# Products of a zero tile in the front of an S4 convolution and gated feed-forward kernel

## The chip, the cores and the metric

The kernel runs on one core of one Trainium2 chip. The metric is the device time of one execution in microseconds, as the median of three runs. A core has a matrix engine, TensorE (PE in the profile; its loading of the stationary operand is shown apart, as PEld), a vector engine (VectorE, DVE), an activation engine (ScalarE, ACT), a general engine (GpSimd, POOL) and an engine that here only starts transfers (SyncE, SP). They work side by side and wait for one another through semaphores. TensorE writes into PSUM, a small memory that DVE and ACT then empty; all else lies in SBUF, the on-chip working memory, and is loaded and stored by DMA. The profile also records which share of its full clock TensorE was granted.

## What is computed

The input is one sequence of 2048 tokens with 640 channels. Six modulation rows come from a small vector c. The first half of the block is a long convolution over the sequence (an S4 layer) on the normalised input, the second a gated feed-forward layer:

```
mod = silu(c) @ w_mod                    # six rows of 640: sa, ca, ga, sb, cb, gb
h = layernorm(x) * (1 + ca) + sa
K[d, l] = Re( sum_n C[d,n] * exp(dt[d] * A[d,n] * l) * dt[d] * B[d,n] )
y = causal_convolution(h, K) + h * Dskip # by FFT over 4096 points in the reference
x = x + ga * y
h = layernorm(x) * (1 + cb) + sb
x = x + gb * ((silu(h @ w1) * (h @ w3)) @ w2)
```

A, B and C are complex and have 128 states for each channel. w1 and w3 are 640 x 1728, w2 is 1728 x 640. All numbers are float32.

## The kernel before

The convolution is done as a transform in two stages over 32 x 64 points, with constant tables (s1r, s1, s2, i1, i2) as operands of matrix products. The kernel has three stretches.

**The front.** First come the parameters. `polar` (lines 236 to 296) turns A, B, C and dt of 128 channels, and later of the other 512, into exponents and phases; it turns its tables over by products with a unit matrix (L285) into `lx`. `mod_early` (line 305) is called eight times. Each call takes up to 256 columns of w_mod: `mod_sums` multiplies them by silu(c) on TensorE (L303, four column groups of 32), DVE copies the sums out (L311), TensorE turns the row into columns (L313), and DVE copies these into `cols` (L314). `mod_shift` (line 316) then makes the shift of the first layer norm: two groups of products (L327, L336) and their copies (L328, L338).

For each of the sixteen tiles of 128 tokens `ln1_norm` normalises the tile and `u_stage1` (line 413) does the first stage of the transform: products of 32 rows by 64 columns (L430), in every other tile also products of one row (L422) for the shift, into two PSUM tiles `pu`, one with the tag Z, one with A or B. ACT or DVE empties the first (L435), DVE the second (L436), and SP stores the result in the scratch `us` (L437).

Meanwhile the convolution's kernel K is made, in 40 steps of 16 channels. A step s consists of the phases on POOL (L487 to L489), absolute value, cosine and sine on ACT, exponents from TensorE (L451, tile `pa`) through ACT's exponential, real and imaginary tables on DVE (L516 to L527), the sum over the states on TensorE (`kgen`, L540, tile `pk`), its scaling on DVE (`k1evac`, L547 and L548), and the first stage of its transform on TensorE (`k_stage1`, L558, tile `pt`), which ACT copies out. The front runs ten rounds of a loop over these steps, `kgen` of step 0 to 8 among them.

**The rounds.** Behind the front the steps of K and the second stage (`stage2`, L589), the products in the frequency domain (L606 to L614) and the inverse (`inverse1`, L631) run in an order written out by hand, the string ROUND, with the flag `in_order[0]` set: each instruction is then held behind the one traced before it on its engine.

**The feed-forward layer** follows, with weights split into two parts of fewer bits and seven instead of eight block products. Its instructions are recorded by a helper and all carry L108. Between the convolution and this layer stands `keep_warm`: 10 and 18 products of a zero tile called `idle`, 128x128 by 128x512, into PSUM that nothing reads.

What sets the order in the front is a planner: it simulates the engines and issues what is ready first, except for what is pinned. `tc.keep_in_program_order` pins one instruction behind the one traced just before it on the same engine; what is traced after it is not pinned by that. ACT's instructions in the front are pinned, TensorE's are not. The planner also makes the waits: a tile in PSUM that is read waits for everything traced before that writes into its bank. A tile with a tag and one buffer waits for the readers of its predecessor with the same tag: Z, A and B serve `pu`, `pa`, `pT` and others, pk the sums of K, pb the `pt`, and pk and pb in turn the sums of `mod_early`.

The tile `dz`, 128 x 160, is cleared by DVE at the very start (L164). Later SP loads the 640 numbers of Dskip into four of its 128 rows (L765), and `k1evac` adds it to the sums. The products of the change read its first 128 columns as the stationary operand and its columns, 160 at most, as the moving one.

Of the kernel before, what the change touches and what calls it, by code (L numbers as in the profile page):

```python
# [9 lines left out]
F32 = mybir.dt.float32  # L10
# [7 lines left out]
P = 128  # L18
L = 2048
D = 640  # L20
F = 1728
NA, NB = 32, 64
DC = 128
NDC = D // DC
SD = 16
# [65 lines left out]
def bc(ap, axis, n):  # L91
    v = ap.unsqueeze(axis)
    shape = list(v.shape)
    shape[axis] = n
    return v.broadcast_to(shape)
# [18 lines left out]
def tile_kernel(ctx: ExitStack, tc: tile.TileContext, a):  # L114
    nc = tc.nc
    V, S, G, PE = nc.vector, nc.scalar, nc.gpsimd, nc.tensor
# [16 lines left out]
    in_order = [False]  # L133

    def keep(ins):

        return tc.keep_in_program_order(ins) if in_order[0] else ins
# [5 lines left out]
    def acopy(out, in_):  # L143
        return tc.keep_in_program_order(S.copy(out, in_))  # L144
# [17 lines left out]
    gaT = kp.tile([P, D // 4], F32, name="gaT")  # L162
    dz = kp.tile([P, D // 4], F32, name="dz")
    V.memset(dz, 0.0)  # L164
    sc = kp.tile([P, KD], F32, name="sc")
    one4 = kp.tile([P, 1], F32, name="one4")
    cT = kp.tile([P, KD], F32, name="cT")
# [2 lines left out]
    psS = ssm.enter_context(tc.tile_pool(name="psS", bufs=1, space=PSUM))  # L170

    tz = ctx.enter_context(tc.tile_pool(name="tz", bufs=4, reuse_waits="tile"))
    tabs = ExitStack()
    tp = tabs.enter_context(tc.tile_pool(name="tp", bufs=2, reuse_waits="tile"))
    once = lambda shape, dt, name: tp.tile(shape, dt, name=name, bufs=1)
# [122 lines left out]
    def mod_sums(w, pm):  # L298

        n = w.shape[2]  # L300
        for k in range(KD):
            g = slice(k % 4 * NA, k % 4 * NA + NA)
            keep(PE.matmul(pm[g, :n], sc[:, k:k + 1].broadcast_to([P, NA]), w[:, k, :], start=(k < 4), stop=(k > 0), tile_position=(0, g.start)))  # L303

    def mod_early(i, w, tag):

        pm = psS.tile([P, 512], F32, name="pm", tag=tag, bufs=1)
        n = w.shape[2]
        mod_sums(w, pm)
        part = flat[2 * (i % 2)][:, 6 * D:]  # L310
        V.tensor_copy(part[:, :n], pm[:, :n])  # L311
        for b in range(n // P):
            PE.matmul(pm[:, 256 + b:257 + b], part[:, b * P:(b + 1) * P], one4, start=True, stop=True)  # L313
        V.tensor_copy(cols.rearrange("p s k -> p (s k)")[:, 2 * i:2 * i + n // P], pm[:, 256:256 + n // P])  # L314

    def mod_shift():

        sa, ca, ga, zero, inv, r, gs = (cols[:, i] for i in range(7))
        V.tensor_scalar(ca, ca, 1.0, None, op0=OP.add)
        V.tensor_scalar(zero, ca, 0.0, 1e-18, op0=OP.is_equal, op1=OP.mult)  # L320
        V.tensor_tensor(ca, ca, zero, op=OP.add)
        V.reciprocal(inv, ca)
        V.tensor_tensor(r, inv, sa, op=OP.mult)

        pr = psS.tile([P, 2, 512], F32, name="pr", tag="Z", bufs=1).rearrange("p a b -> p (a b)")
        for k in range(KD):
            PE.matmul(pr[:64, k * P:(k + 1) * P], r[:, k:k + 1].broadcast_to([P, 64]), ident, start=True, stop=True)  # L327
        V.tensor_copy(rrow[:64], pr[:64, :D])  # L328
        rc = hpz.tile([P, 4, D // 2], F32, name="u")[:, 0].rearrange("p (k c) -> p k c", k=KD)
        V.tensor_tensor(rc, bc(c1, 1, KD), bc(r, 2, 2 * NA), op=OP.mult)  # L330
        ps = psS.tile([P, 512], F32, name="ps", tag="pk", bufs=1)
        for k in range(KD):
            for hh in range(2):
                lo, hi = max(k * P, hh * 320), min(k * P + P, hh * 320 + 320)
                if lo < hi:
                    PE.matmul(ps[hh * 64:hh * 64 + 64, lo - hh * 320:hi - hh * 320], rc[:, k],  # L336
                              ident[:, lo - k * P:hi - k * P], start=True, stop=True, tile_position=(0, hh * 64))
        V.tensor_copy(shift, ps[:, :320])  # L338

    def mod_gate():  # L340
# [72 lines left out]
    def u_stage1(j):  # L413


        x = xt[j]
        u = hpz.tile([P, 4, D // 2], F32, name="u", bufs=2)
        pu = [psS.tile([P, 2, 512], F32, name="pu", tag=t, bufs=1) for t in ("Z", "AB"[j % 2])]
        one = j % 2 == 0
        for q in range(2 if one else 0):  # L420
            for hh in range(2):
                PE.matmul(pu[0][hh * 64:hh * 64 + 64, q, :320], c1[q * NA:q * NA + 1],  # L422
                          rrow[q * NA:q * NA + 1, hh * 320:hh * 320 + 320],
                          start=True, stop=False, tile_position=(q * NA, hh * 64))
        for h in range(2):
            for q in range(2):
                r0 = (2 * h + q) * NA
                r = slice(r0, r0 + NA)
                for hh in range(2):
                    PE.matmul(pu[h][hh * 64:hh * 64 + 64, q, :320], s1r[r], x[r, hh * 320:hh * 320 + 320],  # L430
                              start=not (one and h == 0), stop=True, tile_position=(r0, hh * 64))
        if one:
            acopy(u[:, :2, :], pu[0][:, :, :320])
        else:
            V.tensor_tensor(u[:, :2, :], pu[0][:, :, :320], bc(shift, 1, 2), op=OP.add)  # L435
        V.tensor_tensor(u[:, 2:, :], pu[1][:, :, :320], bc(shift, 1, 2), op=OP.add)  # L436
        nc.sync.dma_start(usw[:, 4 * j:4 * j + 4, :], u)  # L437
# [95 lines left out]

    def kgen(s):
        E, A = EC.pop(s), AA.pop(s)
        pk = psS.tile([P, SD // 4, NB], F32, name="pk", tag="pk", bufs=1)
        for g in range(SD // 4):
            for st, x in enumerate((E, A)):
                for dq in range(4):
                    keep(PE.matmul(pk[dq * 32:dq * 32 + 32, g, :], x[:, g * 4 + dq, 1, :], x[:, g * 4 + dq, 0:3:2, :],  # L540
                                   start=(st == 0), stop=(st == 1), tile_position=(0, dq * 32)))
        PK[s] = pk

    def k1evac(s):
# [178 lines left out]
    def conv_part(fn):  # L723
        return lambda k: fn((k - LAG) // 8, (k - LAG) % 8)

    parts = {"PH": phases, "AB": absph, "CO": cosine, "SI": sine, "PA": lambda k: exp_fast((k,)), "XA": fast,
             "PQ": lambda k: exp_slow((k,)), "XQ": slow, "E1": real1, "E2": real2, "A1": imag1, "A2": imag2,
             "kg": kgen, "K": k1evac, "pt": k_stage1, "uk": k_out}
    conv = {"st": conv_part(stage2), "kc": conv_part(k_copy), "T": conv_part(products), "Y": conv_part(sums),
            "iv": conv_part(inverse1), "zt": conv_part(z_store)}  # L730
# [30 lines left out]
    for i, t in enumerate(("pb", "pk", "pb", "pk", "pb")):  # L761
        mod_early(i, wm[i], t)
# [4 lines left out]
    for j in range(4, 7):  # L767
        ln1_load(j)
    nc.sync.dma_start(prm[:, :, d1], prma[:, :, d1])
    mod_shift()  # L770
    exps(0)
    ln1_norm(0)
# [3 lines left out]
    for n in ("AB", "CO", "SI"):  # L776
        do(n, 0)
    u_stage1(0)
    u_stage1(1)
    ln1_norm(2)  # L780
    for i, t in enumerate(("pb", "pk", "pb")):
        mod_early(5 + i, wg[i], t)
    mod_gate()
    u_stage1(2)
    u_stage1(3)
    rest = polar(d1, G)
# [61 lines left out]
    for rnd in range(NS // EB):  # L848
        if 2 <= rnd < 7:
            late_load(rnd - 2)  # L850
        for word in ROUND:
            name, k = word[:2].rstrip("+-"), EB * rnd + int(word[len(word[:2].rstrip("+-")):])
# [51 lines left out]
    V, S, G, PE = (InOrder(tc, e, (in_order,)) for e in (V, S, G, PE))  # L904
# [544 lines left out]
```

## Time and profile before

| | us |
|---|---|
| median of three runs | 998.04 |
| the three runs | 998.29, 992.06, 998.04 |
| the profiled execution's own time | 1000.31 |
| its span, first to last instruction | 998.5 |
| PE, DVE, ACT, POOL busy in the span | 911.9, 737.4, 535.6, 340.6 |
| mean granted clock of TensorE over the span | 0.94 |

A line of the profile gives the start, the busy time, the engine, the source line, the operation, out and in by the program's names, and the shapes; brackets hold how long the engine was idle before and what ended that. A row of the view by stretches gives the stretch, its length, the busy time of each engine with its count of instructions, the granted clock, the mean busy share of the 16 DMA engines, and GB/s. A row of the view of waits gives the engine and line that waited, for whom, and then the sum, the number and the longest of the waits. A product of float32 numbers appears as two records. Ends of matrix products are modelled, their starts are not.

### The profile page before, as it was taken

What the parts mean: (1) busy time and instruction counts of PE and PEld (TensorE: products, weight loads), DVE (VectorE), ACT (ScalarE), POOL (GpSimd) and SP (SyncE); (2) the same over time, 40 slices, a digit from 0 to 9 for tenths busy, and PEclk for the clock granted to TensorE, in tenths of its full rate; (3) what the DMA queues carried; (4) which work ended last, traced back from release to release, by engine and by line L of the source; (5) the groups of instructions that cost most, each with busy time, mean ns of one, the idle gap of its engine ahead of it and who ended that gap; (6) DMA issues with size and microseconds to landing.
All of it is one profiled execution on the core that took longest, in us unless ns stands there. A gap on an engine that the chain in (4) does not pass through costs nothing.

```text
span 998.5 us, 19955 instructions
## 1 busy us (share of the span) xinstructions
PE 911.9 (91%) x7924; PEld 681.0 (68%) x7924; DVE 737.4 (74%) x1224; ACT 535.6 (54%) x732; POOL 340.6 (34%) x310
## 2 busy tenths in 40 slices
PE   5777788999989997889999999989899999999998
PEld 2434545666666665567888888666678888888786
DVE  4588868999999975678566676687796666676765
ACT  4559468999999942356333333354643333333332
POOL 1541242455544300323222233354342222224441
PEclk9956757999999999999999999999999999999999
DMA  9462264667765788691211104979231111123352
GB/s 261 151 246 89 117 152 137 170 198 209 196 182 173 207 198 246 204 280 48 92 54 54 53 28 118 253 217 280 69 131 54 54 54 53 53 87 99 93 200 76
DMA packets 103568, 140.67 MB, mean 141 GB/s; under 512 B 20564, under 2 KB 62676, under 8 KB 103476
## 3 DMA queue, kind: packets, MB, share of 16 engines
q1 hardware_dynamic: 92692, 113.58, 39.3%
q10 hardware_dynamic: 8480, 18.09, 6.1%
q0 software_dynamic: 2304, 7.74, 2.3%
q8 instruction: 62, 1.02, 0.4%
q14 instruction: 30, 0.25, 0.1%
HBM read 107.92 MB, written 31.46 MB: 140 GB/s over the span
## 4 chain that ended last, share of the span: by engine, by line
PE 43%; DVE 4%; DMA 3%; ACT 2%; issue 2%; POOL 1%; SPq 0%; DVEq 0%; ACTq 0%; POOLq 0%
PE ps L108 43%; DMA A<-zs 1%; DMA xm<-in_x_dram 1%; DVE ul L108 1%; DVE T L108 1%; DVE xm L108 1%; ACT s L108 1%; ACT gh L108 1%; DVE s L108 1%; SPq L108 0%; DMA rw<-in_w_dram 0%; DVE gl L108 0%; POOL s L108 0%; POOL S L108 0%; ACT T L108 0%
## 5 line engine op out<-in xcount | busy, mean ns | idle before, releaser
L108 DVE TENSOR_TENSOR s<-ps,s 128x512 f32<-128x512 f32 x138 | 94.7, 687 | 77.4 <-PE ps L108 77.0
L108 DVE TENSOR_TENSOR gl<-rw,gh 128x640 fp32r<-128x640 f32 x87 | 83.2, 957 | 61.5 <-ACT gh L108 59.4
L108 ACT CAST gh<-rw 128x640 fp32r<-128x640 f32 x87 | 63.2, 727 | 115.9 <-PE ps L108 85.4
L108 POOL TENSOR_TENSOR rw<-rw,gbr 128x512 f32<-128x512 f32 x56 | 84.5, 1515 | 106.0 <-DMA rw<-in_w_dram 87.7
L589 PE MATMUL p<-uk,s 128*64 128x256 f32 x640 | 82.3, 401 | 16.3 <-DMA s<-in_s_dram 7.1
L108 POOL TENSOR_TENSOR S<-rw 128x256 f32<-128x256 f32 x46 | 35.6, 777 | 176.2 <-DVE S0l L108 159.3
L487 POOL TENSOR_TENSOR ph<-thi,iota 128x1376 int32<-128x1376 int32 x20 | 51.0, 2552 | 128.5 <-DVE A L527 94.7
L108 PE MATMUL ps<-xA,gh 128*128 128x512 f32 x280 | 89.0, 396 | 0.7 <-ACT xA L108 0.4
L108 PE MATMUL ps<-gh,uh 128*128 128x512 f32 x224 | 89.6, 400 | 0.0
L108 PE MATMUL ps<-gl,uh 128*128 128x512 f32 x224 | 89.2, 398 | 0.0
L108 PE MATMUL ps<-gh,ul 128*128 128x512 f32 x208 | 82.7, 397 | 0.0
L141 ACT ACTIVATE A<-pa 128x1024 f32<-128x1024 f32 (+1 forms) x80 | 64.5, 814 | 26.5 <-PE pa L451 26.1
L589 PEld LDWEIGHTS p<-uk,s 128*64 128x64 f32 x640 | 46.6, 142 | 43.1 <-issue 10.0
L108 PEld LDWEIGHTS ps<-xA,gh 128*128 128x128 f32 x280 | 52.9, 190 | 14.1 <-ACT xA L108 1.0
L558 PE MATMUL pt<-s,K 128*64 128x128 f32 x640 | 52.9, 306 | 4.6 <-ACT uk L144 4.6
L523 DVE TENSOR_TENSOR A<-A,ph 128x1024 f32<-128x1024 f32 x40 | 55.6, 1391 | 0.9
L108 PE MATMUL ps<-xA,gl 128*128 128x512 f32 x140 | 55.3, 395 | 0.2 <-DVE gl L108 0.2
L516 DVE TENSOR_TENSOR E<-A,cs 128x1024 f32<-128x1024 f32 x40 | 51.2, 1281 | 0.3 <-ACT cs L141 0.3
L540 PE MATMUL pk<-E 128*32 128x64 f32 x1280 | 45.3, 237 | 6.1 <-DVE E L519 5.1
L558 PEld LDWEIGHTS pt<-s,K 128*64 128x64 f32 x640 | 40.7, 152 | 13.7 <-ACT uk L144 7.6
L108 PEld LDWEIGHTS ps<-gl,uh 128*128 128x128 f32 x224 | 43.3, 193 | 9.5
L108 PEld LDWEIGHTS ps<-gh,uh 128*128 128x128 f32 x224 | 42.9, 192 | 9.1
(230 smaller groups left out, 2283.2 us busy)
## 6 DMA issues: line engine op xcount, KB each, us to landing
rw<-in_w_dram ACTq DMA_DIRECT2D x44, 320.0 KB
us<-u SPq DMA_DIRECT2D x16, 640.0 KB
s<-in_s_dram SPq DMA_DIRECT2D x40, 256.0 KB
i<-in_i_dram SPq DMA_DIRECT2D x40, 256.0 KB
rw<-in_wg_dram SPq DMA_DIRECT2D x31, 320.0 KB
rw<-in_wu_dram SPq DMA_DIRECT2D x28, 320.0 KB
uk<-us SPq DMA_DIRECT2D x32, 256.0 KB
zs<-zt SPq DMA_DIRECT2D x32, 256.0 KB
```

The lines of the kernel that those rows point to most:

```text
L108: ins = fn(*args, **kw)
L141: return tc.keep_in_program_order(S.activation(*args, **kw))
L487: hold(G.tensor_tensor(p[:, :, b0:], bc(thi[:, sl], 2, NPG - b0), bc(iota, 1, 2 * SD), op=OP.mult))
L516: keep(V.tensor_tensor(EC[s][:, :, 1:3, :], AA[s][:, :, 1:3, :], mid(cs[s]), op=OP.mult))
L523: keep(V.tensor_tensor(A[:, :, 1:3, :], A[:, :, 1:3, :], mid(ph[s]), op=OP.mult))
L540: keep(PE.matmul(pk[dq * 32:dq * 32 + 32, g, :], x[:, g * 4 + dq, 1, :], x[:, g * 4 + dq, 0:3:2, :], start=(st == 0), stop=(st == 1), tile ...
L558: keep(PE.matmul(pt[c * 64:c * 64 + 64, g, :], kk[:, g, :], s1[:, c, :], start=True, stop=True, tile_position=(0, c * 64)))
L589: keep(PE.matmul(p2[par * 64:par * 64 + 64, pi, c, :], s2[:, pi * 2 + par, c * 64:c * 64 + 64], uk[:, 0:kn + 1:kn, f, :], start=True, stop ...
```

## The change

A helper `idle_products(ps, n)` issues n products of `dz` by `dz` on the whole array into the columns given, each pinned behind what TensorE was given before it. It is called at five places: 24 times on a PSUM tile of its own ahead of all other work; twice in each `mod_early`, four times in `mod_shift`, twice for each of the two tiles in `u_stage1`, and four times (steps 0 to 4) or seven times (steps 5 to 8) in `kgen` while the order is the planner's. In each of these the columns belong to the PSUM tile that has just been written, but to a part of it that no other instruction writes or reads. In `kgen` the tile `pk` is made as large as a bank so that it has such columns.

```diff
+    def idle_products(ps, n):
+
+        for _ in range(n):
+            tc.keep_in_program_order(PE.matmul(ps, dz[:, :P], dz[:, :ps.shape[1]], start=True, stop=True))
...
+    idle_products(psS.tile([P, 2, 512], F32, name="warm", tag="Z", bufs=1)[:, 0, :D // 4], 24)
...
         mod_sums(w, pm)
+        idle_products(pm[:, 320:320 + D // 4], 2)
         part = flat[2 * (i % 2)][:, 6 * D:]
         V.tensor_copy(part[:, :n], pm[:, :n])
...
+        idle_products(ps[:, 320:320 + D // 4], 4)
         V.tensor_copy(shift, ps[:, :320])
...
+        for h in range(2):
+            idle_products(pu[h][:, 1, 320:320 + D // 4], 2)
         if one:
             acopy(u[:, :2, :], pu[0][:, :, :320])
...
-        pk = psS.tile([P, SD // 4, NB], F32, name="pk", tag="pk", bufs=1)
+        pf = psS.tile([P, 512], F32, name="pk", tag="pk", bufs=1)
+        pk = pf[:, :SD // 4 * NB].rearrange("p (g b) -> p g b", b=NB)
...
+        if not in_order[0]:
+            idle_products(pf[:, 256:256 + D // 4], 4 if s < 5 else 7)
         PK[s] = pk
```

## The prediction

> **What bounds the kernel now.** I read the page first, its slices above all: they show where the granted clock is low.
>
> ```profile
> span 998.5 us, 19955 instructions
> ...
> PEclk9956757999999999999999999999999999999999
> ```
>
> Each slice is 25 us. The clock is below full in slices 3 to 7, up to 175 us, and full behind. So whatever the change can win lies in the first sixth of the span; the rest is only moved. The second view is busy time by stretch: the opening, the rest of the front, the rounds written out by hand.
>
> ```profile
> 0.00:38.30 38.30, 24.17 (x111) 14.10 (x112) 18.77 (x64) 15.68 (x23) 8.30 (x12) 1.00 0.85 260
> 38.30:165.00 126.70, 97.32 (x1169) 56.42 (x1167) 100.32 (x162) 87.95 (x87) 50.16 (x40) 0.62 0.43 138
> 165.00:430.00 265.00, 240.65 (x4107) 170.26 (x4104) 227.66 (x403) 200.18 (x221) 96.09 (x67) 0.98 0.71 199
> ```
>
> The columns are the length, then busy time of PE, PEld, DVE, ACT and POOL, then clock, DMA share and GB/s. From 38.3 to 165 us DVE is busy 100.3 of 126.7 us and PE 97.3: DVE is the tighter of the two, and its instructions don't get faster with the clock. A faster PE is worth, at most, what DVE waits for it. The third view is therefore DVE's waits, first up to 38.3 us, then to 165 us.
>
> ```profile
> DVE cols L314 <- PE pm L313: 7.6, 5, 2.2
> ...
> DVE uk L311 <- PE pm L303: 3.1, 3, 1.3
> ```
>
> ```profile
> DVE pk L547 <- PE pk L540: 7.5, 2, 3.8
> ...
> DVE T L606 <- ACT kc L144: 3.0, 1, 3.0
> DVE u L436 <- PE pu L430: 2.6, 1, 2.6
> ...
> DVE u L435 <- PE pu L430: 2.3, 2, 2.0
> DVE lt L281 <- PE pT L285: 1.3, 1, 1.3
> DVE gaT L347 <- PE pg L346: 0.9, 1, 0.9
> ```
>
> That is 10.7 us in the opening, and 14.6 us behind it, with 3.0 us more for an ACT copy that itself waits for PE: 28.3 us is the ceiling of the gain.
>
> **What the clock follows.** The kernel already has one place with products of a zero tile (the tile called idle, behind the rounds), and it is the best witness there is.
>
> ```profile
> 406.90:410.30 3.40, 1.85 (x33) 0.86 (x20) 3.04 (x12) 0.29 (x1) 3.40 (x7) 1.00 0.83 259
> 410.30:413.70 3.40, 3.40 (x9) 2.17 (x7) 1.46 (x3) 1.35 (x2) 0.41 (x1) 0.50 0.33 89
> 413.70:420.30 6.60, 5.92 (x51) 4.03 (x50) 3.11 (x16) 0.50 (x1) 1.97 (x3) 1.00 0.41 109
> ```
>
> ```profile
> 409.69 4.08 PE L108 MATMUL ps<-idle 128*128 128x512 f32 x10 [0.98 <-DVE xm L716]
> ```
>
> Behind a stretch of 3.4 us with PE busy 1.85 us the clock falls to 0.50; through the next 3.4 us PE does zero products on 128x128 and nothing else, and the clock is back at 1.00. So zero operands count. In the front it is otherwise:
>
> ```profile
> 52.05:79.35 27.30, 23.57 (x269) 11.62 (x270) 23.59 (x42) 15.17 (x17) 10.46 (x10) 0.50 0.71 258
> 82.77:93.00 10.23, 9.01 (x106) 5.18 (x106) 9.14 (x18) 9.84 (x14) 0.65 (x2) 0.51 0.11 32
> 96.40:110.00 13.60, 10.15 (x76) 5.92 (x79) 8.51 (x19) 6.15 (x9) 2.56 (x4) 0.50 0.45 183
> 110.00:120.30 10.30, 7.38 (x194) 5.46 (x186) 10.30 (x15) 8.22 (x7) 4.05 (x4) 0.99 0.05 18
> 120.30:147.60 27.30, 23.58 (x280) 14.13 (x284) 19.50 (x27) 15.02 (x18) 11.92 (x8) 0.50 0.53 148
> ...
> 151.00:164.70 13.70, 10.57 (x124) 7.87 (x126) 10.52 (x11) 11.54 (x10) 6.45 (x3) 0.51 0.42 135
> ```
>
> PE is busy 23.57 of 27.30 us and stays at 0.50: its work there is mostly 32x64 products (L430). The one long stretch at full clock, from 110 us, comes right behind 3.4 us of 128x128 products (L285, below). I read it as: the gate weighs how much of the array works, not for how long. The Trainium skill, "TensorE: Matmul & The Clock Gate", section "Why this matters for your kernels", advises no PE gaps over about 3 us between bursts; by that advice this stretch should have been at full clock, and the trace disagrees (0.50 at 86% busy).
>
> **The price of a product.** The trace has the same array shape at both clocks:
>
> ```profile
> 106.52 3.36 PE L285 MATMUL pT<-ident,lt 128*128 128x128 f32 x14
> 109.80 0.36 PE L540 MATMUL pk<-E 128*32 128x64 f32 x8
> ...
> 110.98 2.05 PE L285 MATMUL pT<-ident,lt 128*128 128x128 f32 x16 [0.38 <-POOL lt L279]
> ```
>
> ```profile
> 56.93 0.90 PE L346 MATMUL pg<-uk,misc 128*128 128x160 f32 x2
> ...
> 86.61 2.41 PE L430 MATMUL pu<-x,misc 32*64 32x320 f32 x16
> ```
>
> By start to start, 14 records take 3.28 us at 0.50, 0.234 us each; 16 take 2.05 us at 1.00, 0.128 each: full clock multiplies PE's time by 0.55. One call in the code is two records (L346 is one call, x2). A new product has 160 columns against 128: 2 x 160/128 x 0.128 = 0.32 us at full clock, 0.585 at half. The row of its exact shape, 0.90 us alone at half clock with its own latency, is the upper end (0.50 at full). I take 0.32, since the products stand in rows of at least two behind other work.
>
> **The change part by part.** There are 156 products: 24 ahead of all work; 2 in each of eight mod_early, 4 in mod_shift, 4 in each of sixteen u_stage1, and 4 or 7 in nine kgen (48). Of these 24 + 14 fall in the opening, 118 behind it. Each group stands between real products and the copy that empties the same tile, so I let every copy wait for them.
>
> *The first 24* need only the zero tile:
>
> ```profile
> 0.90 0.19 DVE L164 MEMSET dz<- 128x160 f32 x1
> ...
> 31.62 0.16 DVE L314 COPY cols<-pm 128x2 f32<-128x2 f32 x1 [1.72 <-PE pm L313]
> ...
> 36.77 2.45 DVE L405 SCALAR_TENSOR_TENSOR rs<-mv,rs 128x2 f32<-128x2 f32 x1 [1.09 <-POOL rs L404]
> ```
>
> ```profile
> 10.21 1.07 PE L303 MATMUL pm<-uk,sc 128*32 128x256 f32 x4 [10.21 <-DMA uk<-in_w_mod_dram]
> 12.17 2.08 PE L285 MATMUL pT<-ident,lt 128*128 128x128 f32 x8 [0.90 <-DVE lt L281]
> ```
>
> ```profile
> 14.18:31.60 17.42, 16.91 (x79) 8.41 (x78) 6.82 (x16) 5.21 (x6) 4.12 (x3) 1.00 0.97 308
> ```
>
> PE has nothing to do until 10.2 us. With one to two stretches of 3.4 us at half clock, as at 410 us (6 to 12 products), and the rest at 0.32 they end at 10.3 to 11.9 us: up to 1.7 us over the start of the first real product, hidden by the wait for lt until 12.17. The opening's clock column says 1.00, but 8 records of L285 take 2.08 us there, 0.26 each: it really runs at half. At full clock these 2.08 us are 1.1 (gain 0.9), and the 16.91 busy us up to 31.6 become 9.3 plus 10 products at 0.32, 12.5: gain 4.4. DVE's waits for pm (10.7 us) lie in just this stretch, so it passes through. Behind it, from the last cols at 31.62, DVE and POOL set the pace (L405 waits for POOL and then takes 2.45 us itself), so mod_shift's 4 products are hidden, and the gain of its real ones too. **Opening: -5.3**, ends 0 and -10.7. One new wait: the load of D into dz (L765) must follow the products traced before it, and those of mod_shift must follow the load. Nothing stands behind it on SP that is needed before the last mod_early, so I cost it at nothing, and at 2 us for a late landing.
>
> *Behind the opening* PE's 97.3 us split in 77 in the five rows at half clock (52 to 165 us, above) and 20 elsewhere, which I take as full. At full clock throughout: 77 x 0.55 + 20 = 62, plus 118 x 0.32 = 38, together 100. **The products take what the clock gives**: PE's load stays where it was, and only places where DVE waits for few products and much real work gain. u_stage1 is even: 2.41 us for 16 records of L430 at half clock (86.61, above) against 1.3 plus 4 products, 1.3. So I walk DVE's waits:
>
> ```profile
> 136.25:143.60 7.35, 7.35 (x86) 4.67 (x86) 3.81 (x6) 5.05 (x7) 3.23 (x3) 0.50 0.60 170
> 143.64:148.10 4.46, 4.46 (x84) 3.45 (x82) 0.59 (x2) 2.90 (x4) 1.45 (x1) 0.57 1.23 198
> ```
>
> ```profile
> 157.51 1.98 PE L558 MATMUL pt<-s,K 128*64 128x128 f32 x16 [1.87 <-ACT uk L144]
> 160.17 3.68 PE L589 MATMUL p<-uk,s 128*64 128x256 f32 x16 [0.69 <-ACT uk L144]
> ```
>
> ```profile
> 164.52 0.69 DVE L606 TENSOR_TENSOR T<-p,kc 128x512 f32<-128x512 f32 x1 [3.01 <-ACT kc L144]
> ```
>
> The two waits for pk (7.5 us) end a stretch of 11.8 us in which PE is never idle: 6.5 at full clock plus two kgen of 7 products, 4.5: 11.0, gain 0.8. The wait for kc: 5.66 us of PE become 3.1, gain 2.6. The waits for pT and pg (2.2) halve: 1.1. The last kgen of the front, with 7 products behind DVE's last wait, costs 0.5. **Front behind the opening: -4.0**, ends -17.6 (every such wait gone) and +24 (below, at c = 0.5). The rounds are moved as they are: from 165 us the clock is 0.98, and PE and DVE are busy 91% and 86%, so no slack there takes the gain back.
>
> Sum: -5.3 - 4.0 = -9.3. On the profiled execution, 1000.31 us, that is 991.0; it lies 2.3 above the median of the runs, 998.04, from which I forecast **988.7**.
>
> **The rivals.** *The waits go too*: the copies come so much earlier that half of what my sum leaves of the 28.3 us goes as well, 9.5 us: 979. For it: ACT and DVE hand work to PE and back in the front, and a shorter step lets the next start. Against: DVE at 79% busy.
>
> *Only the opening gains*: the clock drops now and then, PE's load rises a little above what it was, and behind the opening nothing is won or some 4 us are lost: 993 to 997. For it: PE's waits for ACT and DVE (29.4 us idle of 126.7) break the stretches up.
>
> *The clock doesn't hold, slower*: all at half clock, PE's load behind the opening would be 77 + 20/0.55 = 113, and 118 x 0.585 = 69, together 182 us; with a cold share c it is 100 + 82c. PE's 126.7 us are full at c = 0.33, and from there PE is the bound of the front; with a third of its idle time, 10 us, that no order avoids, from c = 0.20. Now c is 0.73 (the five rows: 92 us of 126.7). At c = 0.4 the front needs 133 to 143 us, and with the opening's gain the time is 999 to 1009; at 0.5 it is 1007 to 1017. The place is the copies behind u_stage1 and kgen, whose queues on DVE and ACT then stand still. Against it: the products themselves are what brought the clock back at 410 us, and at half clock PE would have hardly a gap.
>
> *The gate counts gaps, not the array*: if time without any product decides, products put straight behind other products fill no gap, the clock stays as it is, and the same sum at c = 0.73 gives 1026 to 1036. The rows at 52 and 410 us speak against it. This is what the advice of the Trainium skill quoted above would give. That the change doesn't do what it says would be the first products falling behind the loads; then the opening's 5.3 us go and it is 994.
>
> **How the numbers follow.** My forecast (983 to 994) 0.45, half of it over 1%; the waits go too 0.22; only the opening, or products that come late, 0.18; slower as the clock falls 0.12; gaps decide 0.03. A difference of 1%, 10 us, is about what a measurement of this kernel can tell from none (its runs lie 992.06 to 998.29). Faster by over 1%: 0.23 + 0.22 = 0.45. Within 1%: 0.22 + 0.18 = 0.40. Slower: 0.12 + 0.03 = 0.15. The range reaches from 975, inside the second case, to 1006, inside the slower one, and leaves out about 0.18.
>
> **What would show it.** Right: granted clock near 1.00 from 5 or 8 us on; L285 at 12 us at 0.13 us a record; the last cols copy near 26 us instead of 31.6; the first L589 near 151 instead of 160.2; DVE's waits for pm below 5 us. Wrong: clock under 0.8 from 38 us on, DVE waiting longer than now for pu and pk, PE over 95% busy in the front. The forecast fails if the order of the work in the front is arranged anew around the products, since I walked the old order.

## The result, and the profile after

Over twenty executions each, the changed kernel takes 1004.42 us in the median and the kernel before 994.91. The ratio is 1.0095, with a 95% interval of 1.0072 to 1.0118: **about 1% slower**. Two executions of the change, 1013.44 and 1017.59 us, count as a slow state and stand outside the ratio. 988.7 was forecast. The time lies within the range that was given only because the range reached into the case of a slower kernel; it lies on the other side of no change from the forecast.

The profiled execution flatters the change: it took 997.45 us, the shortest of the twenty, while the profiled execution of before (1000.31) lies above its own median. Set side by side, the two traces show a gain of 2.9 us that the medians don't. So whatever is read from one trace below is checked against a second trace of the change, or against the ratio of an experiment. First the page of the changed kernel, its span and the clock in 40 slices of 25 us:

```profile
span 995.6 us, 20584 instructions
...
PEclk9888898999999999999999999999999999999999
```

and its busy time by stretch, with the columns explained for before (length; PE, PEld, DVE, ACT, POOL; clock, DMA share, GB/s):

```profile
0.00:38.30 38.30, 31.84 (x206) 23.98 (x206) 23.18 (x73) 13.99 (x22) 13.46 (x16) 0.91 0.78 235
38.30:165.00 126.70, 109.64 (x1451) 77.34 (x1450) 91.95 (x155) 89.40 (x89) 40.61 (x36) 0.89 0.46 150
165.00:430.00 265.00, 238.73 (x4068) 170.13 (x4072) 227.80 (x402) 199.67 (x221) 96.16 (x67) 0.99 0.70 199
```

The clock is better, as meant: from 38.3 to 165 us it is 0.89 where it was 0.62. Since the clock in these traces is either full or half, 0.89 means 2 x 0.11 x 126.7, some 28 us at half, against 96 before. But PE's load isn't what it was: it rose from 97.32 to 109.64 us. Next, the timeline of the changed kernel, the instructions by which the opening is judged (start, busy time, engine and line, tiles, shape, and in brackets the idle time before it and its releaser):

```profile
1.15 9.53 PE L169 MATMUL warm<-dz 128*128 128x160 f32 x48 [1.15 <-DVE dz L164]
11.87 1.16 PE L292 MATMUL pT<-ident,lt 128*128 128x128 f32 x8 [1.18 <-DVE lt L288]
...
26.55 0.16 DVE L322 COPY cols<-pm 128x2 f32<-128x2 f32 x1 [0.23 <-PE pm L321]
...
35.19 0.49 DVE L347 COPY shift<-ps 128x320 f32<-128x320 f32 x1 [0.39 <-PE ps L169]
...
41.08 1.35 PE L169 MATMUL pu<-dz 128*128 128x160 f32 x8
41.78 0.16 DVE L414 SCALAR_TENSOR_TENSOR rs<-mv,rs 128x2 f32<-128x2 f32 x1 [3.05 <-POOL rs L413]
42.37 0.77 PE L439 MATMUL pu<-x,misc 32*64 32x320 f32 x8
...
42.50 0.80 DVE L447 TENSOR_TENSOR u<-pu,shift 128x640 f32<-128x640 f32 x1
...
164.17 0.69 DVE L620 TENSOR_TENSOR T<-p,kc 128x512 f32<-128x512 f32 x1 [1.68 <-ACT kc L144]
```

The shift and the first u copy answer to these two of before (T, the end of the front, started there at 164.52, in a row of the prediction):

```profile
39.87 0.47 DVE L338 COPY shift<-ps 128x320 f32<-128x320 f32 x1
42.91 0.83 DVE L436 TENSOR_TENSOR u<-pu,shift 128x640 f32<-128x640 f32 x1 [2.56 <-PE pu L430]
```

The last cols copy comes 5.1 us earlier, the shift 4.7 us, and the first u copy only 0.4 us. The front ends where it ended before, and behind it nothing much differs: from the first T to the end of the span it is 831.4 us, against 834.0. The second trace of the change, first the same stretch, then its first T:

```profile
38.30:165.00 126.70, 112.30 (x1352) 79.36 (x1352) 90.00 (x154) 83.50 (x85) 40.07 (x36) 0.82 0.46 148
```

```profile
169.76 0.69 DVE L620 TENSOR_TENSOR T<-p,kc 128x512 f32<-128x512 f32 x1 [1.70 <-ACT kc L144]
```

The clock holds less here (0.82), the front ends 5.2 us later than before, and that execution took 1003.32 us, nearer to the median. What engines wait for in the front, in the first trace of the change (DVE, then ACT; sum, number, longest), shows who pays:

```profile
DVE pk L561 <- PE pk L169: 8.7, 3, 5.2
DVE rs L414 <- POOL rs L413: 7.9, 5, 3.1
DVE u L446 <- PE pu L169: 4.7, 4, 2.9
DVE u L447 <- PE pu L169: 2.6, 3, 1.7
```

```profile
ACT u L144 <- PE pu L169: 21.1, 5, 6.8
```

L169 is the line of the new products. These waits for PE now end on them, not on the products that are read. That alone doesn't make the whole of each wait their cost: in the kernel before, DVE waited 7.5 us for pk and ACT 7.9 us for pu, and a kernel with the work in another order and without a single new product, below, has 4.0 and 17.0 us.

### The profile page after: what moved, and what is told of

Same layout as the page of the kernel before. It is cut to its first block, busy times and chain, and to the rows that moved or that the text cites. A ratio compares the mean times of both kernels' runs of the same rounds, so it can differ in the third digit from the quotient of the medians.

```text
span 995.6 us, 20584 instructions
## 1 busy us (share of the span) xinstructions
PE 927.6 (93%) x8236; PEld 709.7 (71%) x8236; DVE 733.4 (74%) x1224; ACT 534.7 (54%) x732; POOL 335.7 (34%) x310
## 4 chain that ended last, share of the span: by engine, by line
PE 68%; ACT 9%; DVE 9%; DMA 7%; issue 3%; POOL 2%; SPq 1%; ACTq 0%; DVEq 0%; POOLq 0%
PE ps L108 45%; PE p L603 6%; PE pt L572 3%; PE pz L645 3%; PE pk L552 2%; PE pa L462 2%; DMA s<-in_s_dram 2%; ACT cs L141 2%; ACT A L141 1%; PE pu L169 1%; DMA A<-zs 1%; DVE ul L108 1%; DVE gl L108 1%; ACT L141 1%; PE pm L310 1%
## 5 line engine op out<-in xcount | busy, mean ns | idle before, releaser
L603 PE MATMUL p<-uk,s 128*64 128x256 f32 x640 | 79.0, 389 | 18.2 <-DMA s<-in_s_dram 5.4
L141 ACT ACTIVATE A<-pa 128x1024 f32<-128x1024 f32 (+1 forms) x80 | 64.2, 815 | 27.3 <-PE pa L462 27.1
L645 PE MATMUL pz<-Y,i 64*128 64x128 f32 x640 | 46.5, 285 | 1.6 <-DVE Y L627 1.6
L645 PEld LDWEIGHTS pz<-Y,i 64*128 64x128 f32 x640 | 38.9, 187 | 12.0 <-issue 8.4
L572 PE MATMUL pt<-s,K 128*64 128x128 f32 x640 | 44.1, 279 | 2.5 <-ACT uk L144 2.5
```

Source lines behind the costliest of these rows:

```text
L141: return tc.keep_in_program_order(S.activation(*args, **kw))
L572: keep(PE.matmul(pt[c * 64:c * 64 + 64, g, :], kk[:, g, :], s1[:, c, :], start=True, stop=True, tile_position=(0, c * 64)))
L603: keep(PE.matmul(p2[par * 64:par * 64 + 64, pi, c, :], s2[:, pi * 2 + par, c * 64:c * 64 + 64], uk[:, 0:kn + 1:kn, f, :], start=True, stop ...
L645: ins = keep(PE.matmul(pz[:, par, (g % 2) * 2 + pi, :], i1[r, pi, c, :], Y[r, pi, c, :], start=(c == 0), stop=(c == 1), tile_position=(par ...
```

## The experiments

The comparison of the two kernels, instruction by instruction, shows that the change is two things. It adds 156 products, and the planner, which simulates them, issues DVE's and PE's other work of the front in another order. So the theories were: **the clock** (the products raise it, and what they cost depends on how long it stays up), **the copies** (each group of products holds up the copy behind it, whatever the clock), and **the order** (gain or loss comes from the planner's new order). Since DVE and PE can be pinned to a recorded order, the parts can be had one by one. All figures stand in one table; "cold" is the time at half clock between 38.3 and 165 us in the one profiled execution, T the start of the first T there. A ratio compares 4 to 12 executions with executions of the kernel before that were taken beside them (20 for the change itself). It is therefore not the quotient of two medians of this table; the two differ by up to 0.3%, and a step of 0.1 or 0.2% between rows is not clear of that.

| kernel | order | products | median us | ratio to before, 95% | cold us | T us |
|---|---|---|---|---|---|---|
| before | old | none | 994.91 | 1 | 95.6 | 164.5 |
| the change | new | all | 1004.42 | 1.0095 (1.0072 to 1.0118) | 27.3 | 164.2 |
| same_again | new | all | 1008.51 | 1.0112 (1.0074 to 1.0149) | 44.4 | 169.8 |
| new_order_alone | new | none | 998.40 | 1.0025 (0.9999 to 1.0051) | 96.2 | 163.7 |
| new_order_opening | new | 24, mod_early, mod_shift | 1000.20 | 1.0038 (1.0015 to 1.0061) | 99.0 | 166.8 |
| new_order_opening_u | new | these and u_stage1 | 1001.24 | 1.0048 (1.0017 to 1.0080) | 41.4 | 162.7 |
| new_order_opening_k | new | opening and kgen | 1005.27 | 1.0089 (1.0059 to 1.0118) | 54.6 | 164.6 |
| n_double_k | new | all, kgen's twice | 1014.47 | 1.0224 (1.0170 to 1.0279) | 30.7 | 175.3 |
| products_old_order | old | all | 1025.58 | 1.0288 (1.0248 to 1.0327) | 66.5 | 191.9 |
| o_opening_k | old | opening and kgen | 998.41 | 1.0045 (1.0015 to 1.0076) | 69.0 | 168.4 |
| o_24_early | old | 24, mod_early | 996.50 | 1.0035 (1.0005 to 1.0066) | 92.0 | 161.3 |
| first24 | old | 24 | 991.63 | 0.9948 (0.9926 to 0.9970) | 99.6 | 162.3 |
| first24_corner | old | 24, on 32x32 | 992.53 | 0.9992 (0.9967 to 1.0018) | 95.6 | 158.6 |
| corner | new | all, on 32x32 | 1048.58 | 1.0516 (1.0456 to 1.0576) | 113.0 | 209.5 |

### The change once more

No edit.

> The changed kernel once more, for a second trace and more times. The profiled execution of the change, 997.45 us, is the lowest of its 20, whose median is 1004.42; the kernel before has 994.91. If the loss lies in stretches where the clock falls (the phase of the gate's window differs from run to run), this trace has more time at half clock between 38 and 165 us than the first (clock 0.89 there) and ends later by about 1.2 us for each 0.01 of clock in that stretch. If the loss is the same in every execution, the clock of the stretch is again 0.89 and the time within 3 us of 1004.

It repeats the result (1.0112), and gave the second trace above. With 0.07 less clock from 38.3 to 165 us its profiled execution took 5.9 us longer, where the first expectation gives some 8; two traces don't settle it.

### Does the array's share set the clock?

All 156 products on 32 rows and 32 columns of the array, with the same number of columns to stream and in the same order:

```diff
-            tc.keep_in_program_order(PE.matmul(ps, dz[:, :P], dz[:, :ps.shape[1]], start=True, stop=True))
+            tc.keep_in_program_order(PE.matmul(ps[:32], dz[:32, :32], dz[:32, :ps.shape[1]], start=True, stop=True, tile_position=(0, 0)))
```

> The change, each product cut to 32 rows by 32 columns of the array with the same 160 moving columns, in the same order. If the gate weighs how much of the array works, the clock falls back to about 0.62 between 38 and 165 us, each product costs about 0.5 us there, and the time is 1020 to 1035 us (ratio 1.025 to 1.04). If the gate only counts time without products, the clock stays at 0.82 to 0.89 and the ratio is that of the change, 1.008 to 1.012.

```profile
38.30:165.00 126.70, 121.40 (x976) 64.22 (x978) 82.67 (x150) 65.68 (x69) 39.20 (x38) 0.58 0.37 130
```

PE is busy 121.4 of 126.7 us, more than in any other kernel, and the clock is 0.58, lower than in any other. The front ends 45 us later, the kernel takes 5.2% more than before. The same number of products on the whole array costs 1%. So a busy PE doesn't raise the clock; a busy array does. At equal products and equal order the raised clock goes with 40 to 44 us (1048.6 against 1004 to 1008). The loss is larger than expected (1.0516; 1.025 to 1.04 was expected).

The mean clock of a whole execution needs care here. Two of the four executions of this kernel have a mean of 0.97, as high as the change, and yet took 1050.24 and 1051.63 us. The profile counts what lies ahead of the first recorded change of the clock as full: in the trace above that is up to 43.9 us, although a product of L169 takes 0.53 us there. If an execution has no rise before the next one, at 142.9 us, then 95.6 us at half clock aren't counted, and the mean would be 0.967. These two executions left no trace, so this stays an estimate.

The fourteen traces together say more than one kernel does. Let each trace up to 170 us be divided into stretches of 3.413 us that begin where its clock changes, and let the columns that PE streams in a stretch be added up, each record weighted by the part of the 128x128 array that it uses (a new product is two records of 160 columns). Of 156 stretches with fewer than 750 such columns, none was followed by a stretch at full clock; of 242 with 1800 or more, none was followed by one at half; the 347 in between went either way. Busy time separates them less well: PE was busy throughout in 330 stretches, and 117 of those were followed by half clock. This was counted after the fact, with the time ahead of the first recorded change taken as half. It fits with the array's share as what counts, and doesn't show why.

### The two halves of the change: order and products

The order alone is the kernel before with DVE and PE pinned in the front to the order that the change's planner chose; the other is the change pinned to the order of before:

```diff
+    order_dve = [...]
+    order_pe = [...]
+    for engine, order in ((mybir.EngineType.DVE, order_dve), (mybir.EngineType.PE, order_pe)):
+        mine = [i for i in traced if i.engine == engine]
+        for before_, then in zip(order, order[1:]):
+            tc.add_manual_dep(mine[then], mine[before_].name, ...)
```

> No product at all, but VectorE's and TensorE's instructions of the front pinned to the order that the change has. Order theory: at least as slow as the change, ratio 1.008 to 1.020, since the clock is low too. Copies theory: as the kernel before, ratio 0.997 to 1.003.

> All 156 products, but VectorE's and TensorE's other instructions of the front pinned to the order of the kernel before. Order theory (the planner put the front in another order, and that order is worse): the products then gain as forecast, ratio 0.985 to 0.995. Copies theory (each copy waits for the products ahead of it, whatever the order): as slow as the change, ratio 1.005 to 1.015.

The order without a single product, in its timeline:

```profile
12.41 2.08 PE L285 MATMUL pT<-ident,lt 128*128 128x128 f32 x8 [12.41 <-DVE lt L281]
14.42 3.62 PE L303 MATMUL pm<-uk,sc 128*32 128x256 f32 x20
...
20.04 0.61 PE L313 MATMUL pm<-one,uk 128*128 128x1 f32 x4
...
26.41 0.16 DVE L314 COPY cols<-pm 128x2 f32<-128x2 f32 x1 [0.64 <-PE pm L313]
...
41.62 1.22 DVE L405 SCALAR_TENSOR_TENSOR rs<-mv,rs 128x2 f32<-128x2 f32 x1 [4.16 <-POOL rs L404]
...
43.46 0.82 DVE L436 TENSOR_TENSOR u<-pu,shift 128x640 f32<-128x640 f32 x1
```

The last cols copy is at 26.4 us here too. In the new order PE waits until 12.4 us, then the products of L285 and twenty of L303 stand in one piece, and behind them the clock is full: four products of L313 take 0.61 us, where in the order of before they took 1.02 (at 16.89 us, in this row) and their clock stayed at half:

```profile
16.89 1.02 PE L313 MATMUL pm<-one,uk 128*128 128x1 f32 x4
```

So the gain of the opening was a gain of the clock, but **the order brings it without the products**. And the order takes it back in the same stretch: it puts `rs` of the next two tiles ahead of the first u copy on DVE, and that waits 4.16 us for POOL (3.05 in the change), which is at its phases. The ratio of the order alone is 1.0025, no gain and no loss that is clear of noise. The order also changes who waits between 38.3 and 165 us, DVE for pk less and ACT for pu more than before (7.5 and 7.9 us there):

```profile
DVE pk L547 <- PE pk L540: 4.0, 2, 3.6
```

```profile
ACT u L144 <- PE pu L430: 17.0, 5, 5.1
```

With all products in the order of before, the order by which the prediction walked, the loss is 2.9%, not a gain of 0.9%. That is outside of what either theory expected. The front ends 27 us later. Where, is seen at 57 us, first the stretch, then the timeline of it:

```profile
57.00:84.30 27.30, 23.82 (x160) 13.73 (x160) 11.61 (x21) 7.20 (x6) 3.73 (x5) 0.50 0.35 124
```

```profile
58.27 1.34 PE L441 MATMUL pu<-x,misc 32*64 32x320 f32 x8
59.55 2.50 PE L171 MATMUL pu<-dz 128*128 128x160 f32 x8
...
62.09 0.82 DVE L449 TENSOR_TENSOR u<-pu,shift 128x640 f32<-128x640 f32 x1 [4.33 <-PE pu L171]
...
62.97 1.35 PE L441 MATMUL pu<-x,misc 32*64 32x320 f32 x8 [0.92 <-DVE u L449]
```

Eight records of real products, 1.34 us; then the four zero products (eight records) at half clock, 2.50 us; only then the copy, for which DVE has stood 4.33 us; and PE's next products for the same tile wait for that copy. The chain from copy to products to copy is closed, and the clock is at half through 27.3 us with PE busy 87% of it. DVE's waits for pu in this kernel's front, and below it ACT's:

```profile
DVE u L449 <- PE pu L171: 19.9, 6, 4.5
```

```profile
ACT u L144 <- PE pu L171: 30.4, 4, 14.3
```

### Which products cost, in the new order

The products were added group by group, with the order held: the call in `u_stage1`, that in `kgen`, or both left out; then kgen's number doubled.

```diff
-        for h in range(2):
-            idle_products(pu[h][:, 1, 320:320 + D // 4], 2)
...
-        if not in_order[0]:
-            idle_products(pf[:, 256:256 + D // 4], 4 if s < 5 else 7)
+        if not in_order[0]:
+            idle_products(pf[:, 256:256 + D // 4], 8 if s < 5 else 14)
```

> The order of the change, pinned, with the products of the opening alone (24, those of mod_early and of mod_shift). With no product this order had ratio 1.0025. Copies theory: the products behind mod_early's sums cost what the clock gives, so 1.000 to 1.004. Clock theory (what counts is the clock of the stretch, the products pay for themselves): 0.993 to 0.998, as for the first 24 alone in the old order (0.9948).

> The same order, the products of the opening and of u_stage1, none in kgen. Copies theory: u_stage1's 64 products make both copies of each tile wait, and the loss of the change (1.0095 to 1.011) is mostly here: 1.006 to 1.010. If kgen's products (7 in a row ahead of a copy that VectorE waits for) are the place: 1.000 to 1.003.

> The same order, the products of the opening and of kgen, none in u_stage1. Copies theory with u_stage1 as the place: 1.000 to 1.004; with kgen as the place: 1.006 to 1.010. If the two only hurt together, since each needs the other's clock, both of these kernels are slower than the change.

> The change with its order pinned, and kgen's products doubled, 8 and 14 in place of 4 and 7: 48 products more, 13 us of PE at full clock, 25 at half. If the time of the change is lost in the runs and stretches in which the clock falls (20 runs of it: 6.8 us more for each 0.01 of mean clock), more products hold it better and pay for themselves: 1.000 to 1.010, cold time between 38.3 and 165 us under 25 us. If the products are themselves the cost, the kgen part of it doubles at least: 1.014 to 1.025.

The order gives 0.25%, the opening's products 0.13% more, u_stage1's 0.10%, kgen's 0.47%, together the 0.95% of the change; each step but the last is within the intervals of its neighbours, and at the last one the intervals still overlap a little. u_stage1's 64 products cost nearly nothing and more than halve the cold time (99.0 to 41.4 us); DVE's waits for pu rise with them from 4.4 to 8.1 us, ACT's stay at 20.8. Their ratio, 1.0048, lies between the two that were expected. kgen's 48 cost 4.7 us, though they take cold time away without u's (99.0 to 54.6 us); with u's they do so in one trace (41.4 to 27.3) and not in the other (44.4). Another 48 cost 1.3% more, 13 us, and bring no more clock (30.7 us cold): 0.27 us for each, nearly the 0.32 us that a product needs at full clock. DVE's wait for pk is the largest of its waits there:

```profile
DVE pk L563 <- PE pk L171: 13.7, 5, 7.1
```

It was 8.7 us with the single number, in both traces of the change, and 4.0, 4.0 and 3.9 us in the three kernels of this order without kgen's products. So each 48 products add about 5 us to this wait. The second of the two expectations holds: the products are themselves the cost, and the copies bear it.

### Which products cost, in the old order

The change pinned to the order of before, without the products of `u_stage1`:

```diff
-        for h in range(2):
-            idle_products(pu[h][:, 1, 320:320 + D // 4], 2)
```

> The order of before, with all products but those of u_stage1 (24, mod_early, mod_shift, kgen). All products in this order gave 1.0288, with DVE waiting 19.9 us for pu; in the order of the change 1.010. If the order of before fails because the copies of u_stage1 then stand behind the products, this kernel gives 1.005 to 1.011, like the same products in the order of the change (1.0089), and DVE waits for pu about 5 us. If it fails because the clock is not held in it, and every product then costs 0.53 us, it gives 1.015 to 1.025 and a cold time of over 60 us between 38.3 and 165 us.

```profile
DVE pk L561 <- PE pk L171: 12.2, 5, 4.2
DVE rs L416 <- POOL rs L415: 4.9, 6, 1.1
DVE u L447 <- PE pu L441: 2.1, 1, 2.1
DVE u L446 <- PE pu L441: 2.0, 1, 2.0
```

1.0045 in place of 1.0288, with as much cold time (69.0 us and 66.5): the loss of 24 us in the old order is u_stage1's 64 products, by way of the copies behind them, and not a clock that holds less. DVE waits 4.1 us for pu, where it was 19.9. From 57.0 to 84.3 us, the stretch shown above, the clock of this kernel is at half too (0.52) and PE as busy (24.41 us), but DVE works 23.14 us instead of 11.61. In the new order the same 64 products cost 0.1%, and DVE waits 7.3 us for pu in the change. The new order has other work of DVE ahead of some copies, as `rs` ahead of the first; that this is what saves them is likely, but was not tested by itself.

### The first 24 alone

All calls but the first left out; then the same 24 on 32 rows by 32 columns (the edit of one line shown above); then the 24 with the two products of each mod_early, in the old order. In all three the order is that of before.

> Only the 24 products ahead of all work; every other instruction stands in the order of the kernel before. By my prediction the opening's gain comes from the clock: with the clock full from about 5 us on and no products behind, the opening gains up to 7 us (4.4 + 0.9 + 3.2 of products left out) if the clock holds through it, about 3 if it falls back after one or two windows. Behind it nothing changes, so 988 to 992 us against 994.9, ratio 0.993 to 0.997. If what the opening gains is given back by waits behind it that don't depend on TensorE, the ratio is 1.000.

> The 24 products ahead of all work, alone and in the order of before, but on 32 rows by 32 columns of the array instead of 128 by 128. Whole-array products in the same places gave 0.9948, a granted clock of full speed from 4.7 to 18.4 us, and a first L606 2.2 us earlier. If that gain comes from the clock, these products give none: the clock is at half up to some 30 us, the ratio 0.999 to 1.002, the last cols copy at 31 to 32 us. If it comes from something else that the products do (an early start of TensorE, the loads of instructions), the ratio is 0.993 to 0.997 again. If 24 products at half clock last longer than the wait for the first load (24 times 0.53 us is 12.6 us), there is a loss of up to 2 us on top, 1.002 to 1.004.

> The order of before, with the 24 products and the two in each of eight mod_early, none in mod_shift, u_stage1 and kgen. The 24 alone hold the clock to 18.4 us. By the prediction's working of the opening, a clock that is held to 32 us takes the last cols copy from 31.6 to 27 us, and if that reaches the end, 0.990 to 0.994. If the copies only wait longer for the products (two at 0.27 to 0.53 us in each of eight calls, 4 to 8 us of PE), the cols copy comes no earlier than with the 24 alone (30.9 us) and the ratio is 0.996 to 1.002.

first24 in its timeline, and its clock by two stretches:

```profile
12.25 1.16 PE L292 MATMUL pT<-ident,lt 128*128 128x128 f32 x8 [2.56 <-DVE lt L288]
...
30.86 0.16 DVE L321 COPY cols<-pm 128x2 f32<-128x2 f32 x1 [1.72 <-PE pm L320]
```

```profile
4.74:18.40 13.66, 9.30 (x72) 7.40 (x71) 10.53 (x33) 7.71 (x15) 3.12 (x2) 1.00 1.10 331
18.40:45.70 27.30, 23.55 (x132) 12.77 (x131) 12.02 (x35) 11.73 (x14) 12.63 (x12) 0.50 0.60 190
```

The clock is up from 4.7 us and falls at 18.4: PE at full clock runs ahead of what it is fed and stands idle for a third of the first stretch. The cols copy comes 0.8 us earlier, not 5.3. On the corner of the array the 24 products last 13.0 us without a gap, and the clock is still at half behind them (L292, 2.08 us):

```profile
1.15 13.00 PE L169 MATMUL warm<-dz 32*32 32x160 f32 x48 [1.15 <-DVE dz L164]
...
14.09 2.08 PE L292 MATMUL pT<-ident,lt 128*128 128x128 f32 x8
...
28.06 0.16 DVE L321 COPY cols<-pm 128x2 f32<-128x2 f32 x1 [0.82 <-PE pm L320]
```

Its cols copy was expected at 31 to 32 us, and is at 28.1, and its T at 158.6, the earliest of all: the clock rose a little later in this execution, behind the twenty products of L303, as in the order alone. Yet its ratio is 0.9992, no gain, while first24 gives 0.9948 (the two intervals just touch). That first24's half per cent comes from the clock is not shown by this: up to 38.3 us the two traces have nearly the same time at half clock, 24.6 us in first24 and 25.3 on the corner, counting what lies ahead of the first recorded change as half. The place of one cols copy in one trace says little about the median. With mod_early's products only 11.0 us are at half there, and the cols copy came at 28.0 us, near the 27 that was expected, but the ratio is 1.0035, higher than either theory expected, though its interval reaches into the second. Its one trace, whose T is 3.2 us early, doesn't show why; this stays open.

**first24 is the one kernel that beats both**, by 0.5% and 1.5%. Where it gains isn't settled: its span, 990.7 us, is 7.8 us shorter than that of before, 2.2 us of it in the front and 5.6 behind it, where nothing was changed.

## Why the prediction was wrong, point by point

*What the clock follows* was right. Zero products on the whole array raise it, products on a corner of it don't, however busy they keep PE. The Trainium skill, "TensorE: Matmul & The Clock Gate", section "Why this matters for your kernels", advises to keep TensorE busy for at least 4 us and without gaps over about 3 us; 13.0 us without a gap on a 32x32 corner left the clock at half, so here the trace disagrees. The rival by which gaps decide is refuted.

*The price of a product* was right: the eight records behind the first u products, from 41.08 to 42.37 us in the change, are 0.32 us for each product, and at half clock four take 2.50 us with their own end, 0.63 each (0.585 and 0.32 were taken). *The first 24* were right: they end at 10.7 us (10.3 to 11.9), L292 takes 1.16 us (1.1), the last cols copy is at 26.55 ("near 26").

*The opening, -5.3* failed, in the step "so it passes through". The 5.1 us are there at the cols copy and are 0.4 at the first u copy, because the order of the work behind had changed; and they weren't the products' in the first place, since the order alone has them. In the old order the 24 products alone gained 0.8 us there: the prediction took the clock to stay up once it was up, but in the trace of first24 PE at full clock ran dry before 18 us, and the clock fell.

*Behind the opening, -4.0* failed in two terms. The first is the cold share, which the forecast took as 0. It is 0.22 in one trace and 0.35 in the other. These two executions have a mean clock of 0.973 and 0.965 over the whole span; the 18 executions that the ratio counts have 0.968, which puts their cold share near 0.30, by an estimate between the two traces. In these 18 the time falls by 5.2 us for every 0.01 of clock (correlation -0.66), which fits with the cold share, but wasn't tested by itself. One way in which the clock drops can be seen in a place where DVE is busy throughout and PE runs out of work, and the next 3.4 us then are at half:

```profile
68.20:71.60 3.40, 0.81 (x8) 0.57 (x7) 3.33 (x9) 0.42 (x1) 1.13 (x2) 1.00 0.48 169
71.60:75.00 3.40, 3.40 (x28) 1.95 (x29) 3.40 (x6) 0.00 (x0) 0.03 (x1) 0.51 0.85 313
```

The products can't help there: they are issued behind real ones, and the array does nothing where PE waits. Of the seven falls between 20 and 168 us in this trace, four come behind a stretch like this one, with PE busy 0.8 to 1.2 of 3.41 us. In the other three PE was busy 2.2 to 2.9 us, so starving is not the only way. The sum 100 + 82c gives 118 and 129 us of PE work for the two traces; 109.6 and 112.3 were measured, so the direction was right and the size too large by 8 to 15%.

The second term is the copies. "u_stage1 is even" holds at full clock alone; at half clock it is 1.34 us of real and 2.50 us of zero products in the rows at 58 us, and in the order by which the prediction walked it cost 24 us, not nothing. The waits for pk were to shrink by 0.8 us from 7.5; they are 8.7 us in the change, and kgen's products cost 4.7 us. Had the order stayed as it was, the forecast would have been wrong by 35 us (1.0288 x 994.9 against 988.7); the planner's order saved the change 19 us of that.

*The rounds are moved as they are* was right, within 3 us.

*The rivals.* What happened is nearest to "the clock doesn't hold, slower", to which 0.12 was given. Its place was right in part (the copies behind kgen, and in the old order those behind u_stage1), and so was the cold share of over 0.20. That PE then is the bound of the front was not borne out: it was busy 109.6 and 112.3 of 126.7 us. Its price, 999 to 1009 us, holds the median, though it was given for a share of 0.4; that is luck in part. The chance for it was too small because the forecast's own numbers, PE idle for 29.4 of 126.7 us behind other engines, were used for "the stretches break up" and then not for the cold share. The condition stated at the end, that the order be arranged anew, was met as well: the order of DVE and PE in the front differs between the two kernels. By itself it cost 0.25%, not clear of nothing, and in it the products cost 0.7% where they cost 2.9% in the old order.

## What to carry to other kernels

Work that only keeps the matrix engine's clock up has its best chance where the engine has nothing else to do and nobody waits behind it: here only the 24 products ahead of all work gained, half a per cent, and no other group did. Put between real products and the copy that empties them, such work is paid by the copy, at twice the price whenever the clock is down (0.63 us in place of 0.32), and it can't stop the clock from falling where the engine is starved. When a planner sets the order, pin the old and the new order and run both with and without the change, or the order's effect is read as the change's.

## What was not expected of the hardware

The clock in an opening hangs on how single stretches of 3.4 us are filled. In the trace of first24 it changes at 4.74, 18.40 and 45.70 us, 4 and 8 times 3.41 us apart. Twenty products of L303 in one piece of 3.62 us raised it in the order alone, with no zero product at all. In before, sixteen of them and then L313 (one column each) filled the same time, and it stayed down. The Trainium skill, "TensorE: Matmul & The Clock Gate", section "What's actually happening", states that this window of 3413 ns runs freely and doesn't start with the kernel. The traces agree: divided by 3.413, the changes at 4.74 us (first24), 57.0 us (all products, old order) and 71.6 us (the change) leave 1.3, 2.4 and 3.3 us. Where the window falls on the work would then be a matter of chance in each execution, which may be why single traces of the front differ by several us (T at 164.2 and 169.8 for one and the same kernel); that was not tested by itself.
